# Batch-0 and batch-1 keys and queries loaded in 128-partition tiles with long runs, and the first w_in group decoded in two column halves

## The chip, the core and the metric

One NeuronCore of a Trainium2 chip runs the whole kernel. TensorE (PE in the profile) multiplies matrices from on-chip memory (SBUF) into accumulator banks (PSUM); VectorE (DVE) and ScalarE (ACT) do everything elementwise; SyncE (SP) issues all the transfers between device memory and SBUF, in order, on one queue. Each engine works through its own instruction list in order and waits on semaphores for the others. The metric is the device time of one execution in microseconds (us), lower is better; where several executions were made, their median.

## What is computed

An attention with a packed set of 32 queries `p`, a second attention of the 576 queries `q` over the packed result, and two dense layers in a row (the first with SiLU, the second with a cosine):

```python
def _attn_ref(q, k, v, p):                     # 8 batches, 8 heads, 576 rows, 64 wide; p has 32 rows
    p_packed = sm_attn(p, k, v)                # softmax(p k^T / 8) v
    out = sm_attn(q, p_packed, p_packed)

x = attn_out.transpose(0, 2, 1, 3).reshape(4608, 512)
h = x @ w_in;  x = (h * sigmoid(h)) @ w_out    # w_in 512 x 2048, w_out 2048 x 512
h = x @ w_in2; out = (h * cos(h)) @ w_out2
```

The four weight matrices come as 64-bit floats and are taken apart on the chip ("decode"). The rows of one batch may be worked on in any order as long as the output rows go to the right places: the kernel uses that.

## The kernel before

The program writes its operations in a logical order and a planner (`Plan`) then orders them for every engine: a list schedule by due times, with a price for each operation (`price`). For a transfer the price is bytes divided by an assumed rate: 232 for the 64-bit weights, 260 for other tiles with runs of 128 elements and more, 150 for the rest. The planner's order is fixed in the program that is built; on the chip nothing is reordered. Where the planned PE would idle between 6 and 60 us, `run` puts in fillers (`busy`, line 1248): small matmuls of the identity into a bank that is free.

The boot is the part up to the first dense layer, for batches 0 and 1 (class `Boot`). Its steps, by the names that the profile shows:

- `load` brings k, q and v into three tiles `bx`: 96 partitions, each with 6 neighbouring rows of each head, so runs of 6 x 64 x 4 = 1536 B. Four transfers of two heads each, for each of the three and each batch.
- `turned` transposes pairs of rows on PE against `ident` (24 transposes of 96 columns for one of k and q of a batch) into PSUM banks and copies them into four tiles `bkt`; `copy` leaves it to the planner whether ACT or DVE does it. The result holds a batch's rows in a permuted order.
- `stage1`: packed queries `pbd` (cut from `pin`) times `bkt` give scores; their maximum `mx`, a copy of the scores `ba`, one exp on ACT, transposes of `ba` into `bat`; `weighted` multiplies `bat` with the values, divides (`bpp`) and transposes once more into `ppf`. There are two head groups, g = 0 and 1.
- `products` multiplies `ppf` with the four decoded tiles `w1e` of the first quarter of w_in, so that w_in is applied to the 32 packed rows rather than to 576 (banks `mb` and `sb`, then split into the two parts of a tile `w`). One `w1_unit` decodes one tile: two steps on ACT, three on DVE, each 128 x 512, on a raw tile `wd` or `wde` of 512 KB.
- `stage2`: scores of the queries `bkt` over `ppf` in the banks `hb` and `acc`; DVE transposes them into `ba`, makes the softmax in halves of 288 rows (ACT does the exps), transposes them back into `bat` and splits them into `a`.
- `first` is the dense layer: hb <- a, w, then the activation into `gf` and `g`, then acc <- g, w, with w_out's tiles (`w_96` and on, decoded from raw tiles through `wy`). With acc <- g PE is in its steady work.

After the first layer of all batches comes the second layer (`second`), whose weights are loaded as products from `w2s` through SP, 7 tiles a step into a ring of 16, and whose rows `output` writes to device memory. Tiles of the permuted batches 0 and 1 are cut there into pieces of neighbouring output rows with a step, at every 96th row.

## Time and profile before

| | us |
|---|---|
| median of 3 runs | 1477.23 |
| the runs | 1475.91, 1480.18, 1477.23 |
| the profiled execution, device time | 1478.51 |
| its span, first to last instruction | 1476.7 |
| PE busy | 1465.8 |
| DVE busy | 1139.9 |
| ACT busy | 761.9 |

The profile is of one execution. Busy time counts an engine's instructions from start to end; matmuls overlap each other, so PE busy isn't PE at its best, and fillers count as busy too. The time of one instruction in a full queue is better read from its start to the start of the next. A transfer's time from issue to landing holds the time that it stood behind others in the queue.

### The profile page before, as it was taken

To read this page: it belongs to the slowest core of one execution; us is meant where nothing else is said; L and a number is where in the kernel's file an instruction comes from. 1 tells how busy PE (TensorE), PEld (TensorE's weight loads), DVE (VectorE), ACT (ScalarE), POOL (GpSimd) and SP (SyncE) were. 2 spreads that over 40 slices of the span, in tenths; PEclk is the share of its full clock that TensorE was granted. 3 is DMA by queue.
4 is the path that set the end of the run, shared out by engine and by line. 5 is a ranking of instruction groups with operands and counts; after the bars stand their busy time and mean duration, and the time that the engine had idled before them with its cause. 6 is when DMAs were issued, how large, how long until landed. Compare 5 with 4: busy or idle time off the path is not lost.

```text
span 1476.7 us, 34030 instructions
## 1 busy us (share of the span) xinstructions
PE 1465.8 (99%) x13100; PEld 1402.8 (95%) x13100; DVE 1139.9 (77%) x2344; ACT 761.9 (52%) x1571; POOL 0.7 (0%) x6
## 2 busy tenths in 40 slices
PE   8999999999999999999999999999999999999998
PEld 6899888899899998999999999999999999999998
DVE  6998787767887687866487778888787877777765
ACT  6976554545456455555354444454454544444443
POOL 0000000000000000000000000000000000000000
PEclk9999999999999999999999999999999999999999
DMA  9776665876867656354777758777676657575560
GB/s 272 210 243 187 163 169 128 242 206 153 215 178 205 208 150 192 129 188 167 268 263 227 228 185 255 230 237 237 214 222 201 215 180 240 182 233 184 191 197 36
DMA packets 313985, 296.52 MB, mean 201 GB/s; under 512 B 172512, under 2 KB 218080, under 8 KB 313824
## 3 DMA queue, kind: packets, MB, share of 16 engines
q1 hardware_dynamic: 313824, 294.35, 66.1%
q8 instruction: 103, 1.69, 0.5%
q14 instruction: 58, 0.48, 0.1%
HBM read 242.81 MB, written 51.45 MB: 199 GB/s over the span
## 4 chain that ended last, share of the span: by engine, by line
PE 96%; DVE 2%; ACT 1%; DMA 0%; issue 0%; SPq 0%; DVEq 0%; ACTq 0%
PE acc L213 54%; PE hb L213 24%; PE mb L213 9%; PE sb L213 9%; DVE rsb L213 0%; ACT ba L213 0%; DMA bx<-in_k 0%; DMA kin<-in_k 0%; DVE ba L213 0%; DVE big L213 0%; ACT bkt L213 0%; DVE wy L213 0%; DVE mx L213 0%; DVE r L213 0%; DVE a L213 0%
## 5 line engine op out<-in xcount | busy, mean ns | idle before, releaser
L213 PE MATMUL acc<-g,w 128*128 128x256 f32 (+2 forms) x3072 | 470.1, 295 | 0.0
L213 PEld LDWEIGHTS acc<-g,w 128*128 128x128 f32 x3072 | 424.7, 188 | 23.4 <-issue 20.5
L213 PE MATMUL acc<-w,g 128*128 128x256 f32 x3456 | 426.7, 276 | 0.0
L213 PEld LDWEIGHTS acc<-w,g 128*128 128x128 f32 x3456 | 408.0, 188 | 0.0
L213 ACT ACTIVATE gf<-hb 128x320 f32<-128x320 f32 (+2 forms) x208 | 95.8, 467 | 103.7 <-PE hb L213 83.4
L213 ACT CAST g<-gf 128x320 fp32r<-128x320 f32 (+2 forms) x194 | 94.4, 488 | 106.1 <-PE acc L213 77.8
L213 DVE TENSOR_TENSOR g<-gf,g 128x320 fp32r<-128x320 f32 (+2 forms) x208 | 108.4, 523 | 46.0 <-PE acc L213 34.2
L213 DVE SCALAR_TENSOR_TENSOR gf<-gf,hb 128x320 f32<-128x320 f32 (+2 forms) x208 | 106.8, 518 | 45.6 <-ACT gf L213 44.4
L213 PE MATMUL hb<-a,w 128*128 128x320 f32 (+2 forms) x768 | 139.9, 298 | 0.6 <-DVE a L213 0.3
L213 PE MATMUL hb<-a,m 128*128 128x320 f32 (+2 forms) x768 | 129.0, 295 | 0.0
L213 ACT ACTIVATE r<-r,half_pi 128x512 f32<-128x512 f32 x144 | 103.7, 720 | 36.9 <-DVE r L213 36.8
L213 ACT CAST g<-r 128x512 fp32r<-128x512 f32 x144 | 89.6, 622 | 61.9 <-DVE r L213 61.7
L213 PEld LDWEIGHTS hb<-a,w 128*128 128x128 f32 x768 | 112.1, 188 | 9.8 <-issue 6.1
L213 PEld LDWEIGHTS hb<-a,m 128*128 128x128 f32 x768 | 109.5, 188 | 7.4 <-issue 5.7
L213 DVE TENSOR_TENSOR g<-r,g 128x512 fp32r<-128x512 f32 x144 | 99.3, 690 | 15.9 <-ACT g L213 15.6
L213 PE MATMUL hb<-w,m 128*128 128x256 f32 x768 | 110.8, 276 | 0.0
L213 DVE SCALAR_TENSOR_TENSOR r<-n,r 128x512 f32<-128x512 int32 x144 | 99.2, 689 | 2.2
L213 ACT ACTIVATE n<-hb 128x512 int32<-128x512 f32 x72 | 43.3, 602 | 108.4 <-PE hb L213 96.5
L213 PEld LDWEIGHTS hb<-w,m 128*128 128x128 f32 x768 | 97.9, 188 | 0.2 <-DVE mb L213 0.2
L213 DVE TENSOR_TENSOR hb<-hb,gf 128x256 f32<-128x256 f32 x72 | 31.1, 432 | 58.0 <-PE hb L213 58.0
L213 ACT ACTIVATE n<-mb 128x512 int32<-128x512 f32 x36 | 21.6, 601 | 82.2 <-PE mb L213 82.1
L213 DVE TENSOR_SCALAR r<-r 128x512 f32<-128x512 f32 x144 | 61.2, 425 | 2.6
(212 smaller groups left out, 1990.7 us busy)
## 6 DMA issues: line engine op xcount, KB each, us to landing
m<-w2s SPq DMA_DIRECT2D x504, 256.0 KB, 3.7
w<-w1dram SPq DMA_DIRECT2D x96, 256.0 KB, 3.7
w2s<-wd SPq DMA_DIRECT2D x28, 512.0 KB, 3.3
wd<-in_moe_w_in SPq DMA_DIRECT2D x24, 512.0 KB, 4.9
wd<-in_moe_w_out SPq DMA_DIRECT2D x20, 512.0 KB, 4.4
raw<-ydram SPq DMA_DIRECT2D x72, 128.0 KB, 3.9
w2dram<-wd SPq DMA_DIRECT2D x16, 512.0 KB, 3.0
w<-w2dram SPq DMA_DIRECT2D x16, 512.0 KB, 5.5
```

The source lines that it names most:

```text
L213: run = lambda: emit(*[real(x) for x in args], **{k: real(x) for k, x in kw.items()})
```

## The change

Four things are changed, and the planner then makes a new order of everything.

1. Keys and queries of batches 0 and 1: one tile `bx` for each, 128 partitions = 8 heads x 16, each with 36 neighbouring rows of one head. Two transfers of 18 rows (4608 B) a partition. The values keep their tile, now called `bv`. `turned` makes 18 transposes of 128 columns for all heads at once, in five copies into one tile `bkt` that holds the rows of each head as (pair, partition). Scores for the packed queries are put back into the order that the values have by the copy (`place`), which writes with a step of 12 elements.
2. The first quarter of w_in: each of the four tiles is loaded, decoded and multiplied in two halves of 256 columns (rows of 2048 B). The second halves are written behind batch 0's softmax in the program.
3. The planner's prices: transfers of weights at 300 instead of 232, tiles with runs of 1024 elements and more at 340, and a price for a 256-column matmul.
4. The outputs of the first two batches: since 16 rows are neighbours now, pieces of 16 rows with a step of 36.

```diff
-            return {64: 30 if k == 96 else 37, 288: 65, 512: 117}[n], 0
+            return {256: 60, 64: 30 if k == 96 else 37, 288: 65, 512: 117}[n], 0
...
-        return self.ISSUE, 4 * math.prod(out.shape) / (232 if out.dtype == I32 else 260 if run >= 128 else 150)
+        return self.ISSUE, 4 * math.prod(out.shape) / (300 if out.dtype == I32 else 340 if run >= 1024 else 260 if run >= 128 else 150)
...
-        wd = rings["wd"]()
+        wd = rings["wd"]()[:, : math.prod(y.shape[1:])]
...
-    def w1_unit(s, hp, w):
+    def w1_unit(s, hp, w, x0=0, x1=512):
         plan.unit = ("w1", s, hp)
 
-        decode(w_in1[hp * P : (hp + 1) * P, 1024 * s : 1024 * (s + 1)], w)
-        DMA.dma_start(w1dram[s, hp], w)
+        decode(w_in1[hp * P : (hp + 1) * P, 1024 * s + 2 * x0 : 1024 * s + 2 * x1], w[:, x0:x1])
+        if x1 == 512:
+            DMA.dma_start(w1dram[s, hp], w)
...
+        @staticmethod
+        def place(a, st):
+            copy(a, st)
...
+        RUN = 16
+        STEP = S // RUN
         chunks = [slice(c, c + CH) for c in range(0, S, CH)]
...
         def __init__(self):
-            self.x = dict(zip("kvq", tiles(bpool, [P, H, NCH, D], F32, "bx", 3)))
-            self.kt = tiles(bpool, [P, S], F32, "bkt", 4)
+            self.x = dict(zip("kq", tiles(bpool, [P, self.STEP, D], F32, "bx", 2)))
+            self.v = tiles(bpool, [P, H, NCH, D], F32, "bv", 1)[0]
+            self.kt = dict(zip("kq", tiles(bpool, [P, H, HALF], F32, "bkt", 2)))
...
-            for g in range(2):
-                for j in range(2):
-                    h = slice(4 * g + 2 * j, 4 * g + 2 * j + 2)
+            if n == "v":
+                for h in range(0, H, 2):
                     DMA.dma_start(
-                        self.x[n][:CH, h].rearrange("r h c d -> r h (c d)"),
-                        src[b, h].rearrange("h (r c) d -> r h (c d)", c=NCH),
+                        self.v[:CH, h : h + 2].rearrange("r h c d -> r h (c d)"),
+                        src[b, h : h + 2].rearrange("h (r c) d -> r h (c d)", c=NCH),
                     )
+                return
+            rows = src[b].rearrange("h (r c) d -> (h r) (c d)", c=self.STEP)
+            for c0, c1 in ((0, self.STEP // 2), (self.STEP // 2, self.STEP)):
+                DMA.dma_start(self.x[n][:, c0:c1].rearrange("p c d -> p (c d)"), rows[:, c0 * D : c1 * D])
...
         def turned(self, src, b, g, bank):
-            x = self.x["k" if src is k else "q"]
-            ts = []
-            for j in range(2):
...
+            n = "k" if src is k else "q"
+            t = self.kt[n]
+            for m0 in range(0, self.STEP // 2, 4) if g == 0 else ():
+                m1 = min(m0 + 4, self.STEP // 2)
+                st = acc[m0 // 4 % 4] if b == 0 else bank()
+                with plan.together():
+                    for m in range(m0, m1):
+                        T.transpose(st[:, (m - m0) * P : (m - m0 + 1) * P], self.x[n][:, 2 * m : 2 * m + 2].rearrange("p c d -> p (c d)"), ident)
+                copy(
+                    t[:, :, self.RUN * m0 : self.RUN * m1].rearrange("p h (m r) -> p m h r", r=self.RUN),
+                    st[:, : (m1 - m0) * P].rearrange("p (m h r) -> p m h r", m=m1 - m0, h=H),
+                )
+            return [t[:, 4 * g + 2 * j : 4 * g + 2 * j + 2].rearrange("p h n -> p (h n)") for j in range(2)]
+
+        def place(self, a, st):
+            copy(
+                a.rearrange("p (w r u) -> p u w r", w=NCH // 2, r=self.RUN),
+                st.rearrange("p (u w r) -> p u w r", w=NCH // 2, r=self.RUN),
+            )
...
-            return lambda c, h2, j: self.x["v"][:CH, 4 * g + 2 * j + h2, 2 * (c % 3) + c // 3, :]
+            return lambda c, h2, j: self.v[:CH, 4 * g + 2 * j + h2, 2 * (c % 3) + c // 3, :]
...
-            copy(a1[:, hf * HALF : (hf + 1) * HALF], st)
+            mem.place(a1[:, hf * HALF : (hf + 1) * HALF], st)
...
-    def products(s, bs, ws=None):
+    def products(s, bs, ws=None, cols=slice(0, 512)):
...
                                 T.matmul(
-                                    bk[64 * j + c : 64 * j + c + 32],
+                                    bk[64 * j + c : 64 * j + c + 32, cols],
...
-                                    ws[2 * kc + j][r],
+                                    ws[2 * kc + j][r, cols],
...
                     m = mslot(b, kc, s)
-                    copy(m[:, 0], bk)
-                    V.tensor_tensor(m[:, 1], bk, f32(m[:, 0]), ALU.subtract)
+                    copy(m[:, 0, cols], bk[:, cols])
+                    V.tensor_tensor(m[:, 1, cols], bk[:, cols], f32(m[:, 0, cols]), ALU.subtract)
...
-        cuts = [p0] + [c for c in range(p0 + 1, p0 + P) if c % (CH if c <= S else HALF) == 0] + [p0 + P]
+        run, step = boot.RUN, boot.STEP
+        cuts = [p0] + [c for c in range(p0 + 1, p0 + P) if c % (run if c <= S else HALF) == 0] + [p0 + P]
...
-                r0, step = n * S + m % CH * NCH + m // CH * 2 + t // 2, NCH
+                r0, by = n * S + m % run * step + m // run * 2 + t // 2, step
             else:
-                r0, step = n * S + t // 2 * HALF + m, 1
-            DMA.dma_start(out[r0 : r0 + (b - a - 1) * step + 1 : step, :], o[a - p0 : b - p0])
+                r0, by = n * S + t // 2 * HALF + m, 1
+            DMA.dma_start(out[r0 : r0 + (b - a - 1) * by + 1 : by, :], o[a - p0 : b - p0])
...
     place_p(0)
-    ws = w1_units(0)
+    ws = [boot_w1() for _ in range(KC)]
+    for hp in range(KC):
+        w1_unit(0, hp, ws[hp], 0, 256)
     boot.load("v", v, 0)
...
-    products(0, (0,), ws)
+    for hp in range(KC):
+        w1_unit(0, hp, ws[hp], 256, 512)
+    for x in (0, 256):
+        products(0, (0,), ws, slice(x, x + 256))
```

Where the planner moves instructions, three places show it. The first rows on SP's queue, that is the order in which the boot's transfers are issued; before (`bx_157` are the keys, `bx_158` the values, `bx_159` the queries, `wd` and `wde` raw weights):

```order
L213 DMA bx_157<-in_k 96x2x384 x2
L213 DMA pin_120<-in_p 32x16x32 x2
L213 DMA bx_157<-in_k 96x2x384 x2
L213 DMA wd_109<-in_moe_w_in 128x1024
L213 DMA wd_110<-in_moe_w_in 128x1024
L213 DMA wde_114<-in_moe_w_in 128x1024
L213 DMA bx_158<-in_v 96x2x384 x2
L213 DMA wde_115<-in_moe_w_in 128x1024
L213 DMA bx_158<-in_v 96x2x384 x2
L213 DMA bx_159<-in_q 96x2x384 x2
L213 DMA bx_157<-in_k 96x2x384 x2
L213 DMA bx_159<-in_q 96x2x384 x2
```

After (`bx_157` keys, `bv_159` values, `bx_158` queries):

```order
L213 DMA bx_157<-in_k 128x1152 x2
L213 DMA pin_120<-in_p 32x16x32 x2
L213 DMA wde_114<-in_moe_w_in 128x512
L213 DMA wde_115<-in_moe_w_in 128x512
L213 DMA bv_159<-in_v 96x2x384 x3
L213 DMA wd_109<-in_moe_w_in 128x512
L213 DMA bv_159<-in_v 96x2x384
L213 DMA wd_110<-in_moe_w_in 128x512
L213 DMA wde_118<-in_moe_w_in 128x512
L213 DMA wde_119<-in_moe_w_in 128x512
L213 DMA bx_158<-in_q 128x1152
L213 DMA wde_116<-in_moe_w_in 128x512
```

The values, and then the queries, are issued behind halves of the weight tiles and no longer behind whole ones and half of batch 1's keys.

On PE, from the weighted sums (`bat`) to the transposes of the queries; L1248 and L1266 are fillers. Before:

```order
L213 MATMUL acc_88<-bx_158,bat_166 32x64 x24
L1248 MATMUL acc_89<-ident 128x64 x2
L213 MATMUL acc_90<-ident,bpp_168 128x128
L1248 MATMUL acc_88<-ident 128x64
L213 MATMUL mb<-w1e_145,ppf_133 32x512 x2
L213 MATMUL mb<-w1e_146,ppf_133 32x512 x2
L1248 MATMUL acc_88<-ident 128x64 x5
L213 MATMUL acc_89<-bx_158,bat_167 32x64 x24
L213 MATMUL hb_92<-ident,bx_159 128x96 x3
L213 MATMUL acc_88<-ident,bx_159 128x96 x3
L213 MATMUL acc_91<-ident,bpp_169 128x128
L213 MATMUL hb_92<-ident,bx_159 128x96 x3
```

After:

```order
L213 MATMUL acc_89<-bv_159,bat_165 32x64 x24
L213 MATMUL acc_88<-bv_159,bat_164 32x64 x24
L213 MATMUL acc_91<-ident,bpp_167 128x128
L1266 MATMUL acc_89<-ident 128x64
L213 MATMUL sb<-w1e_147,ppf_134 32x256 x2
L213 MATMUL sb<-w1e_148,ppf_134 32x256 x2
L213 MATMUL acc_90<-ident,bpp_166 128x128
L1266 MATMUL acc_88<-ident 128x64 x4
L213 MATMUL mb<-w1e_145,ppf_133 32x256 x2
L213 MATMUL mb<-w1e_146,ppf_133 32x256 x2
L213 MATMUL acc_88<-ident,bx_158 128x128 x4
L213 MATMUL acc_89<-ident,bx_158 128x128 x4
```

The second weighted sum stands directly behind the first; the products with w_in come as halves, the second half of a bank behind the first transposes of the queries.

On DVE, the rows up to the first `g` and the subtraction that makes the second part of `w_96`, the first w_out tile; both are read by the first acc <- g. Before:

```order
L213 TENSOR_SCALAR wy_112<-wy_112 128x512
L213 TENSOR_TENSOR w_96<-wy_111,w_96 128x512
L213 SCALAR_TENSOR_TENSOR wy_112<-wy_112,wde_117 128x512
L213 TENSOR_SCALAR rs_128<-sums_126 128x1
L213 SCALAR_TENSOR_TENSOR gf_149<-gf_149,hb_92 128x288
L213 RECIPROCAL rs_128<-rs_128 128x1
L213 SCALAR_TENSOR_TENSOR gf_150<-gf_150,hb_93 128x288
L213 SCALAR_TENSOR_TENSOR wde_118<-wde_118 128x512
L213 TENSOR_SCALAR bpp_168<-sb,rs_127 128x128
L213 TENSOR_TENSOR g_152<-gf_149,g_152 128x288
L213 TENSOR_TENSOR w_97<-wy_112,w_97 128x512
```

After:

```order
L213 SCALAR_TENSOR_TENSOR wy_111<-wy_111,wd_109 128x512
L213 SCALAR_TENSOR_TENSOR gf_149<-gf_149,hb_92 128x288
L213 SCALAR_TENSOR_TENSOR wd_110<-wd_110 128x512
L213 TENSOR_SCALAR rs_128<-sums_126 128x1
L213 TENSOR_SCALAR wy_112<-wy_112 128x512
L213 RECIPROCAL rs_128<-rs_128 128x1
L213 SCALAR_TENSOR_TENSOR gf_150<-gf_150,hb_93 128x288
L213 TENSOR_TENSOR g_152<-gf_149,g_152 128x288
L213 SCALAR_TENSOR_TENSOR wy_112<-wy_112,wd_110 128x512
L213 TENSOR_TENSOR w_96<-wy_111,w_96 128x512
L213 TENSOR_SCALAR bpp_166<-mb,rs_127 128x128
```

The subtraction into `w_96` stood ahead of the first `g` and stands behind it now, and DVE's work for the second w_out tile (`wy_112`, `w_97`) partly behind both.

## Rows read from the trace of the kernel before

**Rows 1.** The profile's page, busy time, share and instructions of PE.

```profile
PE 1465.8 (99%) x13100; PEld 1402.8 (95%) x13100; DVE 1139.9 (77%) x2344; ACT 761.9 (52%) x1571; POOL 0.7 (0%) x6
```

**Rows 2.** What PE waited for from 60 us to the end: us, times, longest.

```profile
PE mb L213 <- DVE r L213: 0.5, 1, 0.5
```

**Rows 3.** Windows (us): busy PE, PEld, DVE, ACT, POOL, granted clock, DMA share, GB/s.

```profile
20.00:25.00 5.00, 4.76 (x81) 3.38 (x81) 2.67 (x5) 2.87 (x7) 0.00 (x0) 1.00 1.08 286
30.00:50.00 20.00, 18.65 (x260) 15.30 (x267) 20.00 (x62) 17.87 (x46) 0.00 (x0) 1.00 1.06 261
```

**Rows 4.** The fillers' line: durations in ns, first and last start in us.

```profile
L1248 PE MATMUL acc<-ident x106: 218/275/323, 10.4 to 44.3; 128*128 128x64 f32 x106
```

**Rows 5.** Windows of one microsecond, same columns; the last is GB/s.

```profile
9.00:10.00 1.00, 1.00 (x19) 0.39 (x17) 0.00 (x0) 0.77 (x2) 0.00 (x0) 1.00 1.01 414
18.00:19.00 1.00, 1.00 (x51) 0.91 (x44) 0.97 (x3) 0.00 (x0) 0.00 (x0) 1.00 1.16 288
33.00:34.00 1.00, 0.94 (x9) 0.80 (x8) 1.00 (x5) 0.71 (x3) 0.00 (x0) 1.00 1.06 241
```

**Rows 6.** Timeline of PE: start, length (us), operation, passes, idle before.

```profile
4.01 1.19 PE L213 MATMUL acc<-ident,bx 96*128 96x96 f32 x6 [4.01 <-DMA bx<-in_k]
...
14.11 1.61 PE L213 MATMUL acc<-ident,ba 128*96 128x128 f32 x12 [0.22 <-ACT ba L213]
...
17.83 0.88 PE L213 MATMUL acc<-bx,bat 96*32 96x64 f32 x48
...
20.53 1.06 PE L213 MATMUL mb<-w1e,ppf 64*32 64x512 f32 x8 [0.18 <-ACT ppf L213]
21.52 1.33 PE L1248 MATMUL acc<-ident 128*128 128x64 f32 x10
22.78 0.88 PE L213 MATMUL acc<-bx,bat 96*32 96x64 f32 x48
23.59 0.47 PE L213 MATMUL hb<-ident,bx 96*128 96x96 f32 x3
...
48.46 0.30 PE L213 MATMUL acc<-g,w 128*128 128x288 f32 x1
...
62.38 3.32 PE L213 MATMUL acc<-g,w 128*128 128x288 f32 x24
65.78 0.53 PE L213 MATMUL hb<-a,w 128*128 128x288 f32 x2
```

**Rows 7.** Timeline of DVE, from the last product to batch 0's softmax.

```profile
26.99 0.69 DVE L213 TENSOR_TENSOR w<-sb,w 128x512 fp32r<-128x512 f32 x1 [2.89 <-ACT w L213]
27.60 0.47 DVE L213 STREAM_TRANSPOSE ba<-hb 128x288 f32<-128x288 f32 x1
...
28.36 0.77 DVE L213 TENSOR_REDUCE mxb<-ba 128x9 f32<-128x288 f32 x2
29.05 0.82 DVE L213 TENSOR_TENSOR ba<-ba,mxb 128x288 f32<-128x288 f32 x2
```

**Rows 8.** DVE's groups up to 60 us: busy us, mean ns, idle before.

```profile
L213 DVE TENSOR_SCALAR wy<-wy 128x512 f32<-128x512 f32 x4 | 1.7, 419 | 0.0
...
L213 DVE RECIPROCAL rsb<-rsb 128x9 f32<-128x9 f32 x4 | 0.8, 204 | 0.0
```

**Rows 9.** Timeline of ACT: score copies, w_in decode, the last exp of stage 1.

```profile
10.88 0.71 ACT L213 COPY ba<-acc 128x288 f32<-128x288 f32 x2
11.46 0.69 ACT L213 ACTIVATE wd<-wd 128x512 int32<-128x512 uint32 x1
12.03 0.67 ACT L213 ACTIVATE w1e<-wd 128x512 f32<-128x512 f32 x1
...
13.93 0.79 ACT L213 ACTIVATE ba<-ba,m 128x576 f32<-128x576 f32 x1
```

**Rows 10.** SP: issue of output transfers (ns min/median/max), and its longest wait, 1100 to 1300 us.

```profile
L213 SPq DMA_DIRECT2D out<-o x54: 332/413/1203, 824.1 to 1473.7; - x54
...
SPq L213 <- PE hb L213: 101.5, 52, 2.3
```

More of the change, by code (lines that the diff above doesn't have):

```diff
@@ L782, in get @@
                 return self.a[g]
-            return cut({"kt": self.kt[2 * g + j], "s": self.a[g], "pp": self.pp[g]}.get(name, self.at[g]), shape)
+            return cut({"s": self.a[g], "pp": self.pp[g]}.get(name, self.at[g]), shape)
         def turned(self, src, b, g, bank):
-            x = self.x["k" if src is k else "q"]
-            ts = []
-            for j in range(2):
-                t = self.get("kt", [P, S], g, j)
-                for h2 in range(2):
-                    st = bank()
-                    with plan.together():
-                        for m in range(3):
-                            pair = x[:CH, 4 * g + 2 * j + h2, 2 * m : 2 * m + 2, :].rearrange("r c d -> r (c d)")
-                            T.transpose(st[:, m * CH : (m + 1) * CH], pair, ident[:CH, :CH])
-                    copy(t[:, h2 * HALF : (h2 + 1) * HALF], st[:, :HALF])
-                ts.append(t)
-            return ts
+            n = "k" if src is k else "q"
[16 more added lines that the diff above has]
+            )
         def values(self, b, g):
-            return lambda c, h2, j: self.x["v"][:CH, 4 * g + 2 * j + h2, 2 * (c % 3) + c // 3, :]
+            return lambda c, h2, j: self.v[:CH, 4 * g + 2 * j + h2, 2 * (c % 3) + c // 3, :]
     ppf = {}
```

## The prediction

> **What bounds the kernel now.** I read the busy shares first: TensorE (PE) is busy 99% of the span [rows 1]. Next, what PE waited for from 60 us to the end: one wait of 0.5 us [rows 2]. So behind the first minute nothing but PE's own work sets the time, and an edit to loads or copies can win only where PE stands or does nothing useful: in the boot. There PE looks busy too, but part of that is filler, the matmuls of line 1248 whose result nobody reads: 106 passes between 10.4 and 44.3 us [rows 4]. Ten of them take 21.52 to 22.78, so 0.126 us each [rows 6] and 13.4 us in all; with the 4.01 us before the first transpose [rows 6] some 17 us of the boot are surely not useful. That is the ceiling of any gain.
>
> The boot has two halves. Up to 27.60 us DVE has gaps (2.67 of 5 us busy from 20 to 25 [rows 3]) and the path is a chain: keys of batch 0, scores, exps (the last starts at 13.93 [rows 9]), weighted sums over the values (17.83 and 22.78), queries transposed from 23.59 [rows 6], their scores. From 27.60, the first transpose of those scores [rows 7], DVE has no gap: 20.00 of 20 us from 30 to 50 [rows 3]. PE starts its first second-layer matmul, acc<-g, at 48.46 [rows 6]; from there its work is packed. [...] The transfers run nearly all the time, but not at one speed: 414 GB/s at 9 us, where only w_in tiles on 128 partitions move; 288 at 18 us, where only 96-partition tiles of k, v and q move; 241 at 33 us, where both kinds are under way [rows 5].
>
> **Transfers.** Keys and queries go from eight loads of 96 partitions with runs of 1536 B to four of 128 with runs of 4608 B, and the first four w_in tiles from rows of 4096 B to two halves of 2048 B. Neither form is in the trace. Bounds: 241 and 414 GB/s. I take 400 for keys and queries and 350 for the halves, because like the fast row they lie on 128 partitions; values stay at 270. By SP's new order 5.5 MB go up to the last query piece: keys 1.2, p 0.1, seven w halves 1.8, values 1.2, queries 1.2. Before it was 6.4 MB, with all of w_in's first group and half of batch 1's keys among it. The first bytes moved at about 2 us; 2.0 + 3.0 + 0.6 + 5.2 + 4.4 + 3.0 = 18.2 us, and some 0.8 to land; at 265 throughout, 23. Before, PE first touched a query at 23.59.
>
> [...]
>
> **The chain to 27.60.** (1) Key transposes: 18 of 128 columns instead of 24 of 96, five copies instead of eight. The last copy ends near 9.0 and the scores of both head groups follow at 9.1. Four half-width decode steps go onto ACT in between; a 512-wide one steps 0.57 us, a 288-wide copy 0.29 [rows 9], so 0.31 each. The copies that put scores back into natural order with a step of 12 on the writing side (new; three on ACT, one on DVE) are not in the trace; I take 0.41, bounds 0.29 (a plain copy) and 0.7. Last exp at 12.5 instead of 13.93. (2) Both weighted sums stand side by side in PE's order, 13.8 to 15.7; before, the second came behind a product and five fillers. They need all four value loads, which the sum above lands by 13. (3) Then PE runs half a product 0.53 (a whole one took 20.53 to 21.52 [rows 6]), four fillers 1.0, half a product 0.53, eight query transposes 1.1 (0.13 each, as 12 in 1.61 us [rows 6]), half a product 0.53, four fillers 1.0, ten transposes 1.3, two fillers 0.5, with 0.8 for two small transposes and a copy that it waits for: 7.3, so 23.0. DVE's first transpose of query scores follows 0.8 later, at 23.8. If I charge every step on DVE and ACT at its listed length instead of its distance to the next (0.69 for 0.61 [rows 7]) the same walk ends at 25.4. I take 24.4, **3.2 us earlier** than 27.60.
>
> Cost of the halves: twelve DVE decode steps become 24. 512 columns step 0.61 and 288 step 0.38 [rows 7], so 0.08 us of a step don't depend on its length: 1.0 us more on DVE, in a stretch where it has gaps. [...]
>
> **From there to packed PE.** In DVE's new order, up to the subtraction into w_96 that the first acc<-g needs, there stand 8 transposes, 12 subtractions or products and 3 steps for gf and g at 0.38; 8 reductions and 4 maxima at 0.345; 4 decode steps and the subtraction at 0.61 [rows 7]; 2 minima at 0.34 and 14 tiny ones at 0.12, which is their listed 0.42 and 0.20 [rows 8] less the same 0.08; and two of 256 columns at 0.35: 19.0 us. I add 1.0 for gaps, bounds 0.3 and 2.0: in ACT's new order full-width w_out decodes stand ahead of exps that DVE waits for. So acc<-g starts at 24.4 + 19.0 + 1.0 = 44.4. PE then has one weighted sum (0.88 [rows 6]) and one small transpose less behind it than before, so 45.4 in before's terms against 48.46: **3.1 us**. A cross-check further on: before, batch 1's first hb<-a started at 65.78, just released, behind 24 acc<-g in 3.4 us [rows 6]. In the new order 14 more acc<-g (2.0 us) stand ahead of it, so it need come only some 1.1 us earlier. The fillers fall from 53 to 46, of two passes each: 1.8 us of PE; the rest has to come from shorter real waits. Gaps that I haven't seen only take away: I put it at **2.9 us**.
>
> Elsewhere. Batch 1's transposes cost PE the same columns. The products of batch 0, four of 256 columns for two of 512, are in the walk. Output rows of the first two batches go out in pieces of 16: 108 output DMAs instead of 54. At 0.41 us each [rows 10] that is 22 us more on SP's queue in the second stage, in front of the w2s loads. I cost it at nothing: SP stood 101.5 of 200 us there waiting for PE to free a buffer [rows 10], and loads are issued 16 buffers ahead at 7 a step.
>
> **The sum.** The profiled execution took 1478.51 us for a span of 1476.7; the median of the three runs is 1477.23, 1.3 lower. 1478.5 - 2.9 = 1475.6, in the median's terms 1474.3, 0.2% less. A measurement of this kernel can tell about 0.3%, 4.4 us.
>
> **Rivals.** (a) More: DVE starts at 23.8, gaps 0.3, and the faster transfers also remove waits that PE's busy time hides. For it: fillers, start and listed waits don't explain all of the 48 us. 4.4 to 6: 1472. 22%.
> (b) The longer runs don't do what they say: mixed with 96-partition values they move at 270. Then values and queries come 1.5 to 3 us later, DVE starts at 26.5, and ACT's copies of batch 1's keys wait in front of batch 0's exps. Against it: w_in did run at 414 before, between slow tiles. About 0.5 us less: 1476.7. 11%.
> (c) Slower: the transfers sink to the 241 of 33 us [rows 5] for the whole boot. The fourth w_out tile, 10.2 MB into the new order, then lands at 45; ACT's queue has its decode at 37, ahead of copies and activations that feed DVE and PE, so they stand 8 us. 8 less the 2.9 is 5 more: 1482. It decides only below some 275 GB/s on average; at 300 the tile is in time. 5%, and in these the case that SP's 54 extra issues make it late by more than the two steps (21 us) that the buffers hold.
>
> **How the numbers follow.** Forecast 62%, (a) 22%, (b) 11%, (c) 5%. With the bounds of start and gaps the forecast itself reaches from 1472.8 (3.1 + 0.6 + 0.7 won) to 1476.1 (3.1 - 1.0 - 1.0). To leave out no more than 2 in 10 the range goes from 1471.2 (inside a) to 1478.2 (all of b). Faster by over 0.3% is (a) and 0.01 of the forecast: 0.23; slower 0.05; within, 0.72.
>
> **What would show it.** The key loads landed by 6 us; windows near 400 GB/s where keys or queries move alone; the two weighted sums side by side before 17; DVE's first score transpose between 23.8 and 25.4; acc<-g between 43 and 46; no wait of PE for w2s loads. I am wrong if DVE starts early but acc<-g doesn't follow (ACT's order), or if PE shows new waits behind 60 us.

## The result: 0.75% slower

The changed kernel takes 1487.45 us (median of 6 runs, 1486.76 to 1492.62) against 1476.92 (6 runs): ratio 1.0075, 95% interval 1.0063 to 1.0088. The prediction said 1474.3, with 5% for slower. The profiled execution took 1492.62 us for a span of 1490.8, 14 us more than the profiled one of before. It is the slowest of the six; the others lie some 11 above, so the trace read below holds some 3 us that the others don't have.

Busy shares of the changed kernel, answering [rows 1], and under it what PE waited for from 60 us on, answering [rows 2] (us, times, longest):

```profile
PE 1471.6 (99%) x13078; PEld 1403.9 (94%) x13078; DVE 1141.5 (77%) x2366; ACT 758.8 (51%) x1561; POOL 0.7 (0%) x6
```

```profile
PE hb L213 <- DVE gf L213: 4.9, 2, 3.2
PE sb L213 <- DMA w<-w1dram: 0.7, 1, 0.7
PE hb L213 <- DVE sb L213: 0.6, 1, 0.6
PE hb L213 <- DVE mb L213: 0.6, 1, 0.6
```

PE is still busy 99%, but the one wait of 0.5 us has become several, and the longest lasts 3.2 us. To see where the time goes I set the two traces of PE against each other: how much later the changed kernel has the same amount of matmul work still before it (fillers left out, each pass weighted by what its kind takes at the mean). It is 2.8 us ahead at 60 us, 1.9 ahead at 120, still some 1 ahead at 260, 9 behind at 300, 12.9 at 600 and 14.3 from 1160 on. (At 260 and 300 the two orders have done different passes, so these two points are good to some 2 us.) So the boot did win, and one stretch from 270 to 290 us lost about three times as much.

**The boot**, timeline of PE in the changed kernel, answering [rows 6] (start, length, passes, idle before):

```profile
4.45 1.97 PE L213 MATMUL acc<-ident,bx 128*128 128x128 f32 x8 [2.31 <-DMA bx<-in_k]
...
7.06 2.11 PE L213 MATMUL acc<-ident,bx 128*128 128x128 f32 x10
...
9.90 1.21 PE L213 MATMUL acc<-bkt,pbd 64*32 64x288 f32 x32 [0.51 <-ACT bkt L213]
...
15.11 1.68 PE L213 MATMUL acc<-bv,bat 96*32 96x64 f32 x96
...
17.39 0.64 PE L213 MATMUL sb<-w1e,ppf 64*32 64x256 f32 x8 [0.18 <-ACT ppf L213]
...
24.53 0.45 PE L213 MATMUL hb<-bkt,ppf 64*32 64x288 f32 x4 [0.44 <-DVE wde L213]
```

```profile
44.74 0.42 PE L213 MATMUL acc<-g,w 128*128 128x288 f32 x2
```

ACT and DVE of the same stretch (the score copies, the last exp; the first transpose of query scores), and windows of 10 us, whose last column is GB/s, answering [rows 9, 7, 3]:

```profile
11.15 1.72 ACT L213 COPY ba<-acc 128x288 f32<-128x288 f32 x3
12.64 0.78 ACT L213 ACTIVATE ba<-ba,m 128x576 f32<-128x576 f32 x1
...
13.39 0.78 ACT L213 ACTIVATE ba<-ba,m 128x576 f32<-128x576 f32 x1
```

```profile
25.52 0.47 DVE L213 STREAM_TRANSPOSE ba<-hb 128x288 f32<-128x288 f32 x1
```

```profile
10.00:20.00 10.00, 9.30 (x187) 6.93 (x188) 8.50 (x32) 9.21 (x26) 0.00 (x0) 1.00 1.05 331
20.00:30.00 10.00, 9.05 (x103) 6.83 (x104) 8.35 (x25) 7.27 (x18) 0.00 (x0) 1.00 1.06 334
30.00:40.00 10.00, 8.69 (x87) 6.90 (x88) 9.95 (x36) 9.50 (x22) 0.00 (x0) 1.00 1.03 335
```

The transfers run at 331 to 335 GB/s where they ran at 256 to 296, and acc<-g starts at 44.74 instead of 48.46.

**The hole**, from 270 to 290 us. First SP's queue: the last of a long row of key and query loads, w_in's products, and the loads of the first two second-layer weight tiles. Then ACT, DVE and PE (in brackets how long the engine stood, and for what):

```profile
263.40 6.82 SPq L213 DMA_DIRECT2D kin<-in_k  x13
270.32 1.96 SPq L213 DMA_DIRECT2D w<-w1dram  x4
272.33 1.42 SPq L213 DMA_DIRECT2D kin<-in_k  x3
273.79 0.93 SPq L213 DMA_DIRECT2D wd<-in_moe_w_in  x2
```

```profile
280.51 0.65 ACT L213 ACTIVATE wd<-wd 128x512 int32<-128x512 uint32 x1 [10.72 <-DMA wd<-in_moe_w_in]
```

```profile
281.19 0.69 DVE L213 SCALAR_TENSOR_TENSOR wd<-wd 128x512 int32<-128x512 int32 x1 [10.39 <-ACT wd L213]
```

```profile
262.54 0.63 PE L213 MATMUL mb<-w,ppf 64*32 64x512 f32 x4
...
263.56 2.03 PE L213 MATMUL acc<-g,w 128*128 128x320 f32 x12
...
268.18 1.07 PE L213 MATMUL hb<-a,w 128*128 128x256 f32 x8
269.09 1.77 PE L213 MATMUL acc<-g,w 128*128 128x320 f32 x11
...
273.18 1.81 PE L213 MATMUL mb<-w,ppf 64*32 64x512 f32 x8 [0.26 <-DMA w<-w1dram]
275.71 1.85 PE L213 MATMUL sb<-w,ppf 64*32 64x512 f32 x8 [0.72 <-DMA w<-w1dram]
277.49 1.88 PE L213 MATMUL acc<-g,w 128*128 128x320 f32 x11
282.54 1.65 PE L213 MATMUL hb<-a,w 128*128 128x256 f32 x6 [3.17 <-DVE gf L213]
283.98 1.00 PE L213 MATMUL acc<-g,w 128*128 128x320 f32 x3
```

The weight tile is issued at 273.79 and lands at 280.5. ACT has its decode next in its list and stands 10.72 us for it; DVE has the next step of that decode and stands 10.39 for ACT; the activations that feed PE are behind both. PE first gets the weights of its products late (two groups of eight, 1.8 us each, where the same two together take 1.0 us from 262.54 to 263.56), then waits 3.17 us for a gf. In the kernel before the same tile was issued at 257.6, and ACT stood 1.81 us for it:

```profile
262.42 0.67 ACT L213 ACTIVATE wd<-wd 128x512 int32<-128x512 uint32 x1 [1.81 <-DMA wd<-in_moe_w_in]
```

Windows of the same place; the third figure from the right is the granted clock:

```profile
279.00:282.00 3.00, 0.37 (x3) 0.10 (x1) 0.81 (x2) 1.49 (x3) 0.00 (x0) 0.98 0.55 101
282.00:285.00 3.00, 2.46 (x11) 2.46 (x12) 3.00 (x6) 3.00 (x7) 0.00 (x0) 0.50 0.58 166
285.00:288.00 3.00, 3.00 (x14) 3.00 (x14) 2.62 (x6) 1.68 (x4) 0.00 (x0) 0.50 0.81 285
288.00:291.00 3.00, 3.00 (x30) 2.86 (x36) 2.17 (x5) 1.37 (x3) 0.00 (x0) 0.89 0.62 186
```

After the pause PE's clock is granted at 0.50 from 282 to 288 us: the six matmuls at 282.54 take 1.44 us to the next row, 0.24 each, where eight of their kind took 0.91 us at 268.18, 0.11 each. So a wait of 3 us cost some 3 more, an estimate: 6 us of work at half the pace.

### The profile page after: what moved, and what is told of

Its sections match the earlier page's. It is cut to its first block, busy times and chain, and to the rows that moved or that the text cites. A ratio compares the mean times of both kernels' runs of the same rounds, so it can differ in the third digit from the quotient of the medians.

```text
span 1490.8 us, 34094 instructions
## 1 busy us (share of the span) xinstructions
PE 1471.6 (99%) x13078; PEld 1403.9 (94%) x13078; DVE 1141.5 (77%) x2366; ACT 758.8 (51%) x1561; POOL 0.7 (0%) x6
## 4 chain that ended last, share of the span: by engine, by line
PE 89%; DMA 4%; DVE 3%; ACT 2%; SPq 1%; issue 1%; DVEq 0%; ACTq 0%
PE acc L213 50%; PE hb L213 22%; PE sb L213 9%; PE mb L213 8%; SPq L213 1%; DMA wd<-in_moe_w_in 1%; DVE r L213 1%; DMA ysb<-ypart 1%; DMA wde<-in_moe_w_in 0%; DVE g L213 0%; DMA ypart<-ysb 0%; DVE w L213 0%; ACT ba L213 0%; DMA w2s<-wd 0%; DVE gf L213 0%
## 5 line engine op out<-in xcount | busy, mean ns | idle before, releaser
L213 PE MATMUL acc<-g,w 128*128 128x256 f32 (+2 forms) x3072 | 478.2, 296 | 0.7 <-ACT g L213 0.4
L213 PE MATMUL mb<-w,m 128*128 128x256 f32 x456 | 63.0, 277 | 0.0
```

The source lines that it names most:

```text
L213: run = lambda: emit(*[real(x) for x in args], **{k: real(x) for k, x in kw.items()})
```

## The experiments

Theories at the start: the planner's new transfer prices cause the hole (P), or any new order would have it (O). Times are medians in us; ratios are against executions of the kernel before made beside them, with 95% intervals.

**1. Prices alone, layout alone.**

```diff
a_oldprice, against the changed kernel
-  ... / (300 if out.dtype == I32 else 340 if run >= 1024 else 260 if run >= 128 else 150)
+  ... / (232 if out.dtype == I32 else 260 if run >= 128 else 150)
b_newprice, against the kernel before
-  ... / (232 if out.dtype == I32 else 260 if run >= 128 else 150)
+  ... / (300 if out.dtype == I32 else 340 if run >= 1024 else 260 if run >= 128 else 150)
```

> The changed kernel with the planner's two transfer prices put back (232 for the weights, 260 for all tiles with runs of 128 and more); layout, halves and output pieces stay. Theory P (price): cheaper weight transfers let the planner put ACT's decode of the first second-layer weight tile closer behind its load, and the 10.7 us that ACT waits for that tile near 270 us come from this. Then the wait falls below 2 us and the time is the 1476.9 of before, less the 2 us won in the boot, plus the 2 us of the output pieces: 1477, bounds 1474 to 1480. Theory O (order): the new layout alone already makes SP run late in the stretch from 160 to 270 us, whatever the price. Then the wait stays at 8 us or more and the time is 1484 to 1489.

> The kernel before with only the two new transfer prices (300 for the weights, 340 for tiles with runs of 1024 and more; none of its loads outside the weights has such runs, so in effect the weights alone). Theory P: the same stall appears, ACT waits 8 us or more for a second-layer weight tile, and the time is 1476.9 plus some 8: 1485, bounds 1481 to 1489. Theory O: no such wait beyond 3 us, 1474 to 1480.

a_oldprice: 1478.18, ratio 1.0005 [0.9996, 1.0014]. b_newprice: 1489.71, 1.0081 [1.0067, 1.0095]. The layout with the old prices is as fast as before; the new prices with the old layout lose all of it. P holds, O falls. In a_oldprice ACT waits 0.8 us for a raw second-layer weight tile; in b_newprice it waits for the first one like this:

```profile
283.74 0.66 ACT L213 ACTIVATE wd<-wd 128x512 int32<-128x512 uint32 x1 [8.77 <-DMA wd<-in_moe_w_in]
```

The same late tile, with none of the change's loads, halves or output pieces. What it costs PE there is spread over more and shorter waits, the longest 1.8 us. Two steps between: a_w260 has 260 for the weights, a_k340 has 232 for the weights and keeps 340 for the long runs.

> The changed kernel with the weights' price at 260 instead of 300, between the old 232 (1478.2) and the new. If the loss grows with the price it is half of it: 1481 to 1484. If there is a point at which the order tips over, it is at one end: 1476 to 1479, or 1486 to 1490.

> The changed kernel with the weights' price put back to 232 and the long runs of keys and queries left at 340. If the weights' price alone causes the loss: 1475 to 1480, no wait of ACT over 3 us for a second-layer weight tile. If the long runs' price has a part in it: over 1481.

a_w260: 1482.70, 1.0041 [1.0027, 1.0054], half of the loss. a_k340: 1483.49, 1.0042 [1.0030, 1.0055]: the long runs' price alone makes that half, so the step of the weights from 232 to 260 adds nothing in a_w260 (both have 340), and the step from 260 to 300 makes the other half. In b_newprice the weights' price alone makes the whole loss: the two prices don't add up.

**2. Is it the tile, or SP's queue?** a_early keeps every engine's order and only issues the two tiles earlier on SP; a_pool keeps it and has POOL issue the stores that stand in SP's queue; a_out1 keeps it and issues the 16-row pieces of a tile as one transfer.

```diff
a_early
+        early = [i for i in seq if self.ops[i].engine == self.DMA and self.ops[i].unit == ("win2", 0, 0)][:2]
+        at = next(x for x, i in enumerate(seq) if self.start[i] >= 236e3)
...
+        seq = [i for i in seq[:at] if i not in early] + early + [i for i in seq[at:] if i not in early]
a_pool
-  DMA.dma_start(dst[dm, :, x : x + t1 - t0], t[:, t0 - k0 : t1 - k0])
+  aside(dst[dm, :, x : x + t1 - t0], t[:, t0 - k0 : t1 - k0])
+  aside = lambda *args: plan.add(plan.DMA, "dma_start", lambda *x, **kw: nc.gpsimd.dma_start(*x, **kw), args, {})
a_out1
+  dst = bass.AP(..., ap=[[2 * DM, (e - a) // run], [step * DM, run], [1, DM]])
+  nc.sync.dma_start(dst, src.resolve())
```

> The changed kernel, every engine's order kept, but for two instructions of SP: the loads of the first two second-layer weight tiles (issued at 273.8 us) stand some 40 issues earlier, at about 245 us. If the wait of ACT for that tile is what costs the stretch from 260 to 282 us, the wait is gone and most of the 8.4 us with it: 1479.5, bounds 1478 to 1482. If SP's lateness would only surface at the next thing (the loads of k behind it, or DVE), the time stays at 1485 to 1488 with a new wait of about the same size.

> The changed kernel, with the order of every engine kept; only the 112 stores of the first layer's sums (ydram and ypart from ysb), which wait in SP's queue for ACT and DVE, are issued by POOL, which does nothing else. Theory L (SP late): in the changed kernel SP's queue issues the loads of 160 to 280 us up to 14 us later than its place in the order was meant, because stores hold it up and because it issues back to back from 166 us on; ACT, DVE and PE then wait for w_in, k and w_in's products in turn. Without the stores SP has some 20 issues (12 us) less before 280 us and no waits on ysb: the loads of the first second-layer weight tiles are issued at 262 us or earlier instead of 274, and 5 to 9 of the 9.7 us lost by 280 us come back: 1480, bounds 1478 to 1483. Theory X (the order on ACT, DVE and PE itself is worse, whatever SP does): 1486 to 1489.

> The changed kernel in the planner's same order, but the pieces of 16 output rows that lie in one tile are issued as one transfer (at the place of the first of them). If SP's extra output issues in front of the loads of ysb are what cost 1.8 us near 1100 us, PE's two waits there (0.64 and 0.58 us) go and the time falls by 1.5 to 2: 1485.7. If the 54 issues are hidden by SP's idle time, as the prediction had it, nothing changes: 1487.4, within 0.5.

a_early: 1487.91, 1.0070 [1.0056, 1.0083]. No gain, though the tile left SP at 247.7: the wait moved. PE now waits for a from the keys' side and for w_in's products:

```profile
PE hb L213 <- ACT a L213: 1.2, 1, 1.2
PE sb L213 <- DMA w<-w1dram: 1.0, 1, 1.0
```

In its profiled execution, one of the two fastest of six, PE was less far behind (3.9 us at 300 us instead of 9.0), and the median of the six shows no gain; the new waits listed are smaller than the old one, so the expected wait "of about the same size" isn't there. The tile is where the lateness shows first, not its cause. a_pool: 1481.22, 1.0023 [1.0013, 1.0032], 6 of the 10.5 us back; in its profiled execution PE is 1.3 us ahead of before at 300 us. With POOL issuing the stores the first tile leaves SP at 267.9 (not 262 as I expected) and ACT waits 5.05 for it instead of 10.72. So SP's queue as a whole is late; every engine's order is the changed kernel's, so it is not the order by itself that loses these 6 us. (Stores from POOL also land later, ypart at 2.6 us at the median instead of 2.2 and ydram at 3.7 instead of 2.6, which may be a part of what doesn't come back.) a_out1: 1488.96, 1.0084 [1.0070, 1.0099], nothing back. What DVE and PE wait for near 1100 us there:

```profile
1097.23 0.23 DVE L213 TENSOR_TENSOR raw<-raw,ysb 128x64 f32<-128x64 f32 x1 [3.25 <-DMA ysb<-ypart]
```

```profile
1098.87 0.99 PE L213 MATMUL hb<-y,m 128*128 128x256 f32 x6 [1.30 <-ACT hb L213]
```

The loads of ysb come late with 60 output issues less, so the 1.9 us or so that the changed kernel loses there are not shown to be the price of those issues. SP itself waits 5.5 us from 1075 to 1100 us in a_out1 for ysb loads to land, a wait that the changed kernel's SP does not have; why they are late in each stays open.

**3. Why is SP late? The price of an issue.** The planner counts 500 ns for each issue on SP. From 180 to 240 us the changed kernel's SP made 103 issues in 60 us, 0.58 each. A load of queries is no dearer than planned, 453 ns at the median (min, median, max; first and last start):

```profile
L213 SPq DMA_DIRECT2D kin<-in_q x64: 311/453/1587, 166.8 to 250.2; - x64
```

The rest are short waits for buffers and for w_in's products; the trace lists 8.2 us of them there, 3.6 in the largest group. Without them it is 0.50 an issue. In the kernel before SP made 105 issues in the same 60 us, so the chip's pace is no other; the plan's is. From 180 to 260 us the plan of the kernel before has 140 issues on SP, that of the change 156: 78 of 80 us at 500 ns. The plan has SP issuing without a pause, so each wait stays as lateness: set beside the traces issue by issue, SP falls from 4.9 to 15.0 us behind its planned times over these 80 us in the change, and from 2.5 to 4.6 in the kernel before. (In the planner SP may issue at most 2.5 us ahead of the transfers, so transfers priced slow hold its issues back.) A higher issue price is then a margin for the waits, not a truer length. a_issue is the changed kernel with one number changed; the three others complete the square of transfer prices and issue price.

```diff
-    ISSUE, WIRE = 500, 650
+    ISSUE, WIRE = 580, 650
```

> The changed kernel, with all its prices, but the planner's price of one issue on SP is 580 ns instead of 500 (103 issues took 60 us from 180 to 240 us in the changed kernel, 0.58 each). Theory L: the planner now leaves SP the time that it needs and starts the loads of 160 to 280 us earlier; no wait of ACT of more than 3 us for a second-layer weight tile; 1474 to 1480. Theory X: a new order, but the same hole: 1484 to 1490.

> The kernel before with nothing but the planner's price of one SP issue at 580 ns instead of 500. If the honest issue price alone is what made the changed kernel with 580 fast (1471.8), this gains as much: 1471 to 1473. If the boot's 2 us belong to the change and the rest to the issue price: 1473 to 1475.5. If the kernel before had slack enough on SP (its first second-layer weight tiles were issued 16 us earlier than the changed kernel's): 1476 to 1479.

> The changed kernel with the old transfer prices (232, 260) and 580 ns for an issue. With old prices and 500 it took 1478.2, with new prices and 580 it took 1471.8. If the new transfer prices do good once SP's issues are priced rightly: 1475 to 1479 here. If they are worth nothing and the issue price is all: 1471 to 1473.

> The kernel before with the new transfer prices (with 500 ns it took 1489.7) and 580 ns for an issue. Theory L (SP late): the loss goes, as it went in the changed kernel: 1471 to 1479, no wait of ACT over 3 us for a second-layer weight tile. Theory X (the new transfer prices make a worse order whatever SP's price, and the changed kernel's recovery was luck): 1484 to 1490.

| transfer prices, issue price | layout before | layout changed |
|---|---|---|
| old, 500 | 1477 (before) | 1478.18 |
| new, 500 | 1489.71 | 1487.45 (the change) |
| old, 580 | 1488.29, 1.0073 [1.0060, 1.0085] | 1487.97, 1.0069 [1.0057, 1.0081] |
| new, 580 | 1476.67, 0.9992 [0.9983, 1.0002] | 1471.82, 0.9962 [0.9949, 0.9974] |

With 580 the changed kernel is 0.4% faster than before. What is left of its waits on PE behind 60 us, and ACT at the place where it stood 10.72 us, with SP's issue of the tile:

```profile
PE acc L213 <- DVE ysb L213: 0.3, 1, 0.3
PE hb L213 <- ACT a L213: 0.2, 1, 0.2
```

```profile
277.15 0.60 ACT L213 ACTIVATE gf<-hb 128x512 f32<-128x512 f32 x1 [0.56 <-PE hb L213]
277.64 0.68 ACT L213 ACTIVATE wd<-wd 128x512 int32<-128x512 uint32 x1
```

```profile
272.18 0.35 SPq L213 DMA_DIRECT2D wd<-in_moe_w_in  x1
```

The tile leaves hardly earlier (272.18), but the order now has its decode later, and ACT takes it without a wait. But the old prices with 580 lose 10 us, which my theory L (room for SP mends it) did not allow. Their hole is another one. PE in b_issue:

```profile
233.29 0.59 PE L213 MATMUL mb<-ident,big 128*128 128x128 f32 x2
234.40 0.63 PE L213 MATMUL mb<-w,ppf 64*32 64x512 f32 x4 [0.52 <-ACT ppf L213]
...
237.61 1.37 PE L213 MATMUL sb<-big,ppf 64*32 64x288 f32 x6 [2.12 <-DVE w L213]
```

```profile
234.00:237.00 3.00, 1.09 (x16) 0.18 (x16) 1.50 (x4) 1.64 (x5) 0.00 (x0) 1.00 0.58 146
237.00:240.00 3.00, 2.39 (x18) 0.93 (x19) 1.73 (x4) 0.11 (x1) 0.00 (x0) 0.65 0.47 78
```

Here no load is late: PE's list holds the weighted sum, the products and the scores of one batch one behind the other with nothing between, and PE waits for each small step in turn. The plan has these gaps itself, 3.9 us up to 237.8 and 7.2 us up to 248.2 of its own time; why it leaves them with dearer issues is not shown. The planner's own start times, which the program works out when it is built, tell the two apart: how far SP's first second-layer weight tile was issued behind its planned time, and how much of PE's planned list behind 60 us is gaps of over 0.3 us.

| kernel | transfers, issue | us | tile behind plan, us | gaps in PE's plan, us |
|---|---|---|---|---|
| a_620 | new, 620 | 1474.33 | 3.2 | 2.5 |
| a_issue | new, 580 | 1471.82 | 4.4 | 0.6 |
| b_newprice_issue | new, 580 | 1476.67 | 5.9 | 0.4 |
| a_oldprice | old, 500 | 1478.18 | 6.3 | 2.0 |
| before | old, 500 | 1477 | 7.6 | 0.4 |
| a_540 | new, 540 | 1475.94 | 10.7 | 0.8 |
| a_k340 | mixed, 500 | 1483.49 | 11.9 | 1.0 |
| a_w260 | mixed, 500 | 1482.70 | 12.3 | 0.4 |
| the change | new, 500 | 1487.45 | 15.3 | 0.8 |
| a_460 | new, 460 | 1496.25 | 16.4 | 1.6 |
| b_newprice | new, 500 | 1489.71 | 19.7 | 1.5 |
| b_old540 | old, 540 | 1476.44 | 3.4 | 5.6 |
| b_issue | old, 580 | 1488.29 | -0.4 | 19.1 |
| a_oldprice_issue | old, 580 | 1487.97 | -1.4 | 20.3 |

So theory M: in the kernel before, transfers priced slow left SP the room that its issue price did not. Cheaper transfers alone make the plan run ahead of SP; dearer issues alone put gaps into the plan itself. From 180 to 260 us the plans of a_issue, b_newprice_issue and a_oldprice have 138, 138 and 142 issues on SP, those of a_w260 and a_k340 152, of b_newprice 156. In the rows with few gaps, the six with the tile less than 11 us behind take 1472 to 1478, the five above 11 take 1483 to 1496; the line at 11 was drawn after these runs, and above it more lateness is not always more time (b_newprice against a_460).

**4. The rule tried on four more kernels**, each with its time forecast from it; a_460, a_540 and a_620 are the changed kernel with that issue price, b_old540 the kernel before with 540.

> The changed kernel with 460 ns for an issue instead of 500 (1487.5) or 580 (1471.8). Theory M (match): two prices decide together. Where the planner's transfers are cheaper than the chip's, SP falls behind its planned places and the engines wait; where they are dearer, the planned order itself has holes on PE. Here the price is cheaper still: SP falls further behind than the 14 to 15 us of the changed kernel at 260 to 270 us, over 18, and the time is 1491 to 1505. Theory Z (any other number gives another order, good or bad by chance): as likely below 1487 as above.

> The changed kernel with 540 ns for an issue. Theory M: between the two neighbours (500: 1487.5, 580: 1471.8), SP behind by 6 to 11 us at 260 us: 1475 to 1482. Theory Z: anywhere from 1470 to 1490.

> The changed kernel with 620 ns for an issue. The planner's own end is now 2.9 us later than with 580, since its order has 2.5 us of holes on PE instead of 0.6. Theory M: SP is behind by less than 3 us, and the time is the 1471.8 of 580 plus 0 to 3: 1471 to 1475. Theory Z: anywhere from 1470 to 1490.

> The kernel before with its own transfer prices (232, 260) and 540 ns for an issue. The planner's own order has 5.6 us of holes on PE behind 60 us (0.4 with 500; 19.1 with 580, which took 1488.3). Theory M: SP is on time, and the holes show as they stand: before's 1477.3 plus 2 to 5: 1479 to 1483. Theory Z: anywhere from 1470 to 1490.

a_460: 1496.25, 1.0112 [1.0089, 1.0134]; a_540: 1475.94, 0.9982 [0.9970, 0.9993]; a_620: 1474.33, 0.9968 [0.9955, 0.9981]: three inside their ranges, though a_460's tile is behind by 16.4 and not by over 18, and a_620's by 3.2 and not by less than 3. Theory Z, an order good or bad by chance, allowed 1470 to 1490 for three of the four and is not ruled out by these runs; against it stand a_pool, which keeps the order, and SP's lateness read issue by issue. b_old540: 1476.44, 0.9983 [0.9970, 0.9996], faster than forecast: 5.6 us of gaps in the plan cost nothing visible, 19 cost 10. The rule says when an order is in danger, not to the microsecond what it costs.

**5. What the change's two parts are worth** at matched prices (new transfers, 580): a_long has the long runs alone, b_halves the column halves alone.

```diff
a_long, against a_issue: the first w_in group whole again
-    ws = [boot_w1() for _ in range(KC)]
+    ws = w1_units(0)
...
+    products(0, (0,), ws)
b_halves, against b_newprice_issue: the halves as in the change
+        w1_unit(0, hp, ws[hp], 0, 256)
...
+        products(0, (0,), ws, slice(x, x + 256))
```

> Matched prices (new transfers, 580 ns an issue): with both parts of the change the kernel takes 1471.8, with neither 1476.7. Here the long runs of keys and queries (and the pieces of 16 output rows) alone, the first w_in group in whole tiles. If the faster loads of keys and queries make the 4.9: 1471 to 1473. If the halves make them: 1475.5 to 1478. Both in part: between.

> Matched prices (new transfers, 580 ns an issue), the loads of keys and queries as before the change on 96 partitions, and the first w_in group in two halves of columns. If the halves make the 4.9 us: 1471 to 1473. If they only cost (24 decode steps for 12 on DVE and on ACT, some 1 us each): 1476.5 to 1478.5.

a_long: 1474.31, 0.9977 [0.9968, 0.9986]; b_halves: 1474.13, 0.9981 [0.9968, 0.9994]. Against 1476.67 with neither and 1471.82 with both, each wins some 2.4, and together they make the 4.9. By the ratios, which are safer between executions made apart, it is 0.15%, 0.11% and 0.30%; the interval of each part alone overlaps that of the kernel with neither, so only the two together are clear of noise. Nor is it all the boot: in the profiled executions PE is at 60 us ahead of before by 1.6 us with neither, 0.4 with the long runs, 2.0 with the halves and 3.3 with both, so the long runs alone win nothing there, and their gain comes with the rest of the new order.

**6. Partitions or run length.** a_short has the changed kernel's order and its 128 partitions, with keys and queries loaded in runs of 1536 B.

```diff
-                DMA.dma_start(self.x[n][:, c0:c1]..., rows[:, c0 * D : c1 * D])
+                    for c in range(c0, c1, 6):
+                        nc.sync.dma_start(self.x[n][:, c : c + 6]..., rows[:, c * D : (c + 6) * D])
```

> The changed kernel in its own order, but each load of keys or queries of batches 0 and 1 goes out as three loads of 384 columns (1536 B a partition, as before the change) on the same 128 partitions. Theory A (partitions): 128 partitions are what makes them fast, so windows in which only keys or queries move stay near 400 GB/s (396 and 415 from 3 to 5 us in the changed kernel). Theory B (run length): they fall to the 288 of the 1536-byte runs before, and DVE's first transpose of query scores (25.5) comes 2 us later or more.

Windows of the key loads (last column GB/s), the changed kernel and then a_short:

```profile
3.00:4.00 1.00, 0.00 (x0) 0.00 (x0) 0.00 (x0) 0.00 (x0) 0.00 (x0) 1.00 1.00 396
4.00:5.00 1.00, 0.55 (x3) 0.55 (x4) 0.00 (x0) 0.00 (x0) 0.00 (x0) 1.00 1.03 415
```

```profile
3.00:4.00 1.00, 0.77 (x4) 0.77 (x5) 0.00 (x0) 0.00 (x0) 0.00 (x0) 1.00 0.93 255
4.00:5.00 1.00, 0.77 (x4) 0.36 (x2) 0.00 (x0) 0.58 (x1) 0.00 (x0) 1.00 0.89 218
```

This is one execution, 1490.18 us. 255 and 218 GB/s against 396 and 415, so 128 partitions alone don't keep these windows near 400, as theory A had it. It isn't shown to be run length either: the median packet of 1536 B took 65 ns from 2 to 5 us, that of 4608 B in the changed kernel 178, hardly less for its bytes (on 96 partitions in the kernel before it was 65 ns in the same window and 94 from 17.5 to 20 us); what slowed a_short's keys were packets that took longer than the median, some 90 ns at the mean from 3 to 4 us, an estimate from the 255 GB/s and the DMA share of 0.93 there. Its queries moved beside w_in halves at 364 and 375 GB/s (16 to 20 us), above the 288 of 96-partition tiles [rows 5], and its six key loads were also six issues on SP, at 0.46 us each for 192 KB. DVE's first transpose of query scores came at 26.44, 0.9 later than in the changed kernel, not 2. So theory B's 2 us isn't there either. Which part is run length and which the extra issues stays open.

## Why the prediction was wrong

**What bounds the kernel.** Right for the kernel before, and used wrongly. "Behind the first minute nothing but PE's own work sets the time" is a property of that order on the chip [rows 2]. The change replaces the order of the whole program, and I kept the sentence for the new one.

**Transfers.** Right: 396 and 415 GB/s for the keys alone (400 taken), 331 to 335 over whole stretches. I took the 400 from the fast row's 128 partitions, whatever the length of the runs. a_short, with 255 GB/s at 128 partitions, disagrees for that stretch, and the measurement decides. Nor do the medians of single packets of 1536 B show that the partitions count: from 2 to 5 us 65 ns on 128 partitions in a_short and 65 on 96 in the kernel before.

**The chain to 27.60.** Last exp at 13.39 (12.5 forecast): the three copies with a step of 12 on ACT take 1.49 us up to the exp behind them, 0.50 each instead of 0.41, and the scores start at 9.90, not 9.1. Weighted sums at 15.11 (13.8); DVE's first transpose at 25.52 (24.4, bounds 23.8 to 25.4). Each step a little late, and the sum 2.1 instead of 3.2.

**From there to packed PE.** acc<-g at 44.74 against 44.4, and the gain at 60 us is 2.8 against 2.9. That it fits so well is in part luck: DVE's first transpose was 1.1 us late, and the way from there took 19.2 us instead of 20.0. That an early acc<-g isn't a gain in itself shows best in b_newprice, where it starts at 41.78 and which is the slowest of the square (PE is some 3 us ahead of before at 48 us there, 1.3 ahead at 60 and 2.0 behind at 90): work that it overtook stands behind it.

**Elsewhere: the step that failed.** I named the price change, read the new order up to 60 us and put everything behind it at nothing. The term that is missing is the lateness of SP's queue: 0.58 us an issue from 180 to 240 us, waits included, against 0.50 in a plan without slack, 15.0 us behind by 260 us. [rows 10] tempted me: SP's idle half is in the second layer, from 1100 to 1300 us; in the stretch from 160 to 280 us I did not look. Of the 13.1 us between forecast and result none is the boot's; the old prices take 9.3 back (1478.18 in a_oldprice), some 1.9 go in the second layer, and the runs of one kernel spread by more than what is left.

**The output pieces** show no cost by their number, as I had it (a_out1), though near 1100 us some 1.9 us go, for a reason that stays open.

**Rivals.** The one on the slower side was a mechanism of the boot (transfers at 241 GB/s), and didn't happen. "PE shows new waits behind 60 us" stood in the text as what would make the prediction wrong; it should have been a rival with a price. The trace of before had the rows for it: SP making some 190 issues from 160 to 270 us, 0.58 each, and ACT's one wait of 1.81 us for the same tile, which says how little slack there was.

## What to carry to other kernels

A cost model's prices work as a set: before one of them is put right, look which other one it offsets, and read how far each queue runs behind its planned times on the chip. A stretch in which an in-order queue issues back to back has no slack, however idle it is elsewhere (SP's here, from 4.9 to 15.0 us behind its plan between 180 and 260 us); a change of order must be followed to that stretch, not only to the place it was made for. Here the same change makes the kernel 0.75% slower or 0.4% faster, as one number of the planner is 500 or 580.

## What the hardware showed that I had not expected

The longest hole in the work of PE was paid twice: after 3.17 us without a matmul the clock was granted at 0.50 for some 6 us (282 to 288 us). In b_issue, behind a wait of 2.12 us, it read 0.65 and 0.78 in the windows from 237 to 243 us. A wait of 1.76 us at 573 us in the changed kernel left it at 1.00. On 128 partitions, keys in runs of 1536 B moved at 218 to 255 GB/s, in runs of 4608 B at 396 to 415.
